# Filler products in the planned gaps of TensorE, a substitution by rows, and held low parts, in a delta-rule attention with two mixture layers

## The chip, the cores and the metric

The kernel runs on one core of one Trainium2 chip. The core has TensorE (PE in the profile, its weight loads PEld), VectorE (DVE), ScalarE (ACT), GpSimd (POOL) and SyncE (SP), which only issues DMAs. The metric is the device time of one execution in microseconds, as a median of several runs; lower is better.

## The reference

Attention by the delta rule over 768 tokens (4 batches, 8 heads, head size 48), then a two-layer network with a leaky ReLU (384 to 2048 to 384), then eight experts (384 to 1024 to 384) whose outputs are weighted by a gate that is normalised by rows and columns in turn.

```python
for t in range(S):                       # attention, per batch and head
    kt, vt, bt = (k_n[:, :, t], v[:, :, t], beta[:, :, t, None])
    y[:, :, t] = np.einsum('bhd,bhde->bhe', q[:, :, t], state)
    v_old = np.einsum('bhde,bhd->bhe', state, kt)
    state = state + bt[:, :, :, None] * np.einsum('bhd,bhe->bhde', kt, vt - v_old)
...
h = x @ w_in                             # first network
x = np.maximum(0.01 * h, h) @ w_out
...
for e in range(E):                       # experts
    h = np.maximum(x @ w1[e], 0.0)
    out += P[:, e:e + 1] * (h @ w2[e])
```

## The kernel before

**Stages.** The 768 tokens are cut into six steps (t = 0 to 5) of 128. For each step and batch b the attention is done in blocks: `part1(t)` normalises the keys and makes the Gram matrix of the step, masked and scaled by beta (tile a, on VectorE, from PSUM); its high half goes to nh (float16, ScalarE), its low half to nl (GpSimd, `tensor_tensor` subtract), and only then GpSimd writes ones on the diagonal of nh (`affine_select`), so nl must be done before that mask. The diagonal 32 x 32 blocks are copied to a_d. `solve(t)` inverts the diagonal blocks of all batches and heads at once on VectorE: it transposes a_d to ld, and for every j multiplies (tile tm) and subtracts (tile xs); in steps 0 and 1 the blocks are 16 wide, so there are 15 such pairs, later 31. A last transpose brings the result to xt (which lies in tile tm). `part2(t, b)` spreads xt into the blocks of a zeroed float16 tile (`spread`: ScalarE, and in step 0 every second block by a VectorE cast), transposes that to a second tile, so that x holds the inverse and u its transpose, and doubles the blocks level by level (s = 16, 32, 64): a product of nh and x, copies p by ScalarE, a product of p and u, copies back into u and x. Then come the products for w, the outputs y and the state.

`main_a(t)` is the first network for the 512 tokens of a step (four batches of 128): 16 slices, each with 9 products x1h/x1l by w into bank ph, leaky ReLUs gh and leak on ScalarE, their difference gl on VectorE, and 9 products into banks po. In step 0 the first four slices (LEAD) run on two batches before the other two are there. `convert` meanwhile brings the weights of the first network into a rounded form by VectorE, ScalarE and GpSimd (tiles raw, cva, cvs, cvp), one piece per slice.

**The order.** All of that (steps 0 to 4 of `main_a`, all six of the attention) is written into a `Recorder`, which doesn't emit instructions but notes them with a cost each (`cost`, L386 on), and then places them: `rank` and `tails` give priorities, attention is favoured by a lead (`AHEAD`), priorities are shaken by random numbers (`SEED`), `place` walks through the engines' queues and takes the best of `ROUNDS` tries; `emit` writes the instructions in the order of their planned starts, and each engine executes in that order. Banks of PSUM are handed out by the plan too (`takes`). In `cost`, the last value marks operations that the plan keeps apart from GpSimd's on VectorE (`shared`). Two loops of products of the zero-filled tile stir into bank ph (`STIR`: 144 and 20) have the lowest rank and are placed wherever PE would idle early on; the tile is later used for maxima. In step 0 the first four subtractions nl are held behind the end of the first solve (`late`, `solved`).

From the last step of the first network on (L1326 and later) another planner orders the work; the change doesn't touch it.

```python
        two = not psum and (method == "tensor_scalar" or len([v for v in src if v.ids.size > 1]) > 1)
...
        for o in late[0:B]:
            o.deps.add(solved[0])
            o.held.add(solved[0])
```

Of the kernel before, what the change touches and what calls it, by code (L numbers as in the profile page):

```python
# [12 lines left out]
F16 = mybir.dt.float16  # L13
# [3 lines left out]
ALU = mybir.AluOpType  # L17
# [3 lines left out]
B, H, S, D = 4, 8, 768, 48  # L21
# [25 lines left out]
SMALL = (0, 1)  # L47

STIR = (145, 20)
AHEAD, EARLY = 60.0, 60.0  # L50
ROUNDS, SEED = 10, 4
NEAR = 0.02
SLACK = 4.0
PAD = 0.07
VTOP = 32.0
# [238 lines left out]
class Recorder:  # L294
# [62 lines left out]
    def cost(eng, method, out, reads, kw):  # L357
# [34 lines left out]
            lat = 0.11 + 0.00073 * n  # L392
        else:
            lat = 0.145 + 0.00104 * m
        two = not psum and (method == "tensor_scalar" or len([v for v in src if v.ids.size > 1]) > 1)
        return lat - 0.08, lat, two

    def rank(self):
# [146 lines left out]
            o.rank = best[1][o]  # L545
        return self.place()

    def emit(self, ordered, hold):
        for o in self.order():
            for fn, args, kw in o.calls:  # L550
                args = [x.real() if isinstance(x, View) else x for x in args]
                o.last = fn(*args, **{k: x.real() if isinstance(x, View) else x for k, x in kw.items()})  # L552
                ordered(o.last)
                for x in o.held:
                    hold(o.last, x.last)
# [3 lines left out]
def delta_moe_kernel(ctx: ExitStack, tc: tile.TileContext, k_l, v_l, q_l, beta_l, wa_in, wg, wc, out):  # L559
# [4 lines left out]
    rec = Recorder()  # L564
# [99 lines left out]
    def spread(t, blk, out, src):  # L664
        if t == 0 and blk % 2:
            dve.tensor_copy(out=out, in_=src)
        else:
            act.activation(out=out, in_=src, func=ACTF.Copy)
# [102 lines left out]
            yield  # L771

    xt_of = {}
    marks, solved = [], []

    def solve(t):
        size = 16 if t in SMALL else 32
# [2 lines left out]
        def blocks(x):  # L780
            return x[:, 0:nd * size * 33].rearrange("p (d r) -> p d r", d=nd)[:, :, 0:size * 32].rearrange(
                "p d (c i) -> p d c i", c=size)[:, :, :, 0:size]
# [3 lines left out]
        xs = a1_p.tile([128, 1056], F32, tag="xs", name="xs")  # L786
        pool.memset(xs, 0.0)
        pool.memset(xs[:, 0:1024:33], 1.0)
        ldb, xsb = blocks(ld).rearrange("p d i c -> p d c i"), blocks(xs)
        yield  # L790
        for j in range(size - 1):
            m = size - 1 - j
            tm = a1_p.tile([128, 1024], F32, tag="tm", name="tm")
            tv = tm[:, 0:nd * (j + 1) * m].rearrange("p (d c i) -> p d c i", d=nd, c=j + 1)
            xv = xsb[:, :, 0:j + 1, j + 1:]
            dve.tensor_tensor(out=tv, in0=ldb[:, :, j:j + 1, j + 1:].to_broadcast([128, nd, j + 1, m]),
                              in1=xsb[:, :, 0:j + 1, j:j + 1].to_broadcast([128, nd, j + 1, m]), op=ALU.mult)
            dve.tensor_tensor(out=xv, in0=xv, in1=tv, op=ALU.subtract)
            if j % 2 == 1:
                yield  # L800
# [5 lines left out]
    def part2(t, b):  # L806
# [15 lines left out]
        xt = xt_of[t]  # L822
        u = at_p.tile([128, H, C], F16, tag="u", name="u")
        x = at_p.tile([128, H, C], F16, tag="x", name="x")
        o = pool.memset(x, 0.0)
        if t == 0 and b < 2:
            behind(o)
        for blk in range(4):
            o = 32 * blk
            spread(t, blk, x[o:o + 32, :, o:o + 32], xt[o:o + 32, :, b * H:(b + 1) * H].rearrange("p j h -> p h j"))  # L830
        dve.transpose(out=u.rearrange("p a b -> p (a b)"), in_=x.rearrange("p a b -> p (a b)"))
        yield
        for s in (16, 32, 64) if t in SMALL else (32, 64):
            pt = p1[b % 2]
# [268 lines left out]
    if True:  # L1103
# [27 lines left out]
        dve.tensor_tensor(out=wg_r[:, :, E:2 * E], in0=wg_f[:, :, 0:E], in1=fr(wg_r[:, :, 0:E]), op=ALU.subtract)  # L1131
        run(solve(0))
        run(part1(1))
        for o in late[0:B]:
            o.deps.add(solved[0])
            o.held.add(solved[0])
        attention(0, 0)
        attention(0, 1)
        ps = phs.tile([128, TB], F32, tag="ph")
        for i in range(2):  # L1140
            for _ in range(STIR[i] // 2):
# [49 lines left out]
            tc.add_manual_dep(ins.ins, before.ins.name, mybir.DependencyInfo(  # L1191
                mybir.DependencyClass.Sync, mybir.DependencyReason.DATA), reason="kept behind")

        rec.emit(ordered, hold)
        pe, act, dve, pool, sp = engines
        ident, ones, wmax, xmax, cmax, wg_f, wg_r, wa, x2_dram = fixed
        x1h, x1l = x1r
# [219 lines left out]
        for c in range(KD):  # L1417
            tag, k = "leak", c % 2

            def emit(c=c, k=k):  # L1420
                o[c] = g_p.slots["leak"][k]
                return [ordered(act.activation(out=o[c], in_=po[c], func=ACTF.Copy))]
# [397 lines left out]
```

## Time and profile before

| | |
|---|---|
| median of 3 runs | 2220.17 us (2218.66 to 2225.01) |
| the profiled execution, time | 2224.42 us |
| its span, first to last instruction | 2222.7 us |
| PE busy | 2108.3 us (95%), 16963 products |
| VectorE busy | 1697.5 us (76%) |
| ScalarE busy | 1399.2 us (63%) |
| GpSimd busy | 607.0 us (27%) |
[...]

The page cuts the span into 40 slices of 55.6 us. PE's busy tenths are 6688 in the first four, 9 or so in the others; the clock's tenths are 8568 in the first four, then 8, 8, and 9 (90% or more) to the end. [...]

### The profile page before, as it was taken

Reading aid. Unit: us, or ns where it says so; the run is one execution under the profiler, and the core shown is the slowest. Engines: PE = TensorE matmul, PEld = TensorE weight load, DVE = VectorE, ACT = ScalarE, POOL = GpSimd, SP = SyncE. Lnnn points to the kernel's source line nnn. Section 1 sums busy time; section 2 is a strip of 40 time slices with the busy share of each in tenths; the row PEclk is TensorE's granted clock in tenths of the full one; section 3 lists DMA queues with packets and bytes.
Section 4 is the critical chain, followed back from the end, with each engine's and each line's share of the span. In section 5 each row is a group of like instructions: output and inputs, shape, how many; then the busy total and the mean of one; then the engine's idle time right before and its main releaser. Section 6 shows DMA issues by size and latency. Waiting matters only on the chain.

```text
span 2222.7 us, 42895 instructions
## 1 busy us (share of the span) xinstructions
PE 2108.3 (95%) x16963; PEld 1585.6 (71%) x16963; DVE 1697.5 (76%) x3313; ACT 1399.2 (63%) x2621; POOL 607.0 (27%) x672
## 2 busy tenths in 40 slices
PE   6688889999999999999999999999999999999999
PEld 4576767787777775767677777777777777777776
DVE  9776687658676467786877877877877878877877
ACT  5868757545656366777666656656656656656554
POOL 3644531103020052345215114214213313312200
PEclk8568889999999999999999999999999999999999
DMA  2456655466655663224333333333333323323321
GB/s 88 141 179 205 220 180 191 167 203 206 200 174 180 220 243 129 108 79 143 114 107 136 115 108 135 115 107 135 115 108 129 121 103 120 123 107 117 112 100 51
DMA packets 123450, 312.85 MB, mean 141 GB/s; under 512 B 14960, under 2 KB 66800, under 8 KB 117104
## 3 DMA queue, kind: packets, MB, share of 16 engines
q1 hardware_dynamic: 121088, 306.18, 40.2%
q10 hardware_dynamic: 2160, 3.93, 0.5%
q8 instruction: 133, 2.18, 0.4%
q14 instruction: 69, 0.57, 0.1%
HBM read 247.84 MB, written 62.13 MB: 139 GB/s over the span
## 4 chain that ended last, share of the span: by engine, by line
PE 75%; DVE 10%; ACT 6%; issue 2%; POOL 2%; DMA 1%; DVEq 0%; ACTq 0%; POOLq 0%; SPq 0%
PE b L1474 25%; PE b L1573 19%; PE ph L1573 10%; PE ph L1474 6%; PE bg L552 5%; PE po L552 4%; PE ph L552 4%; DVE tm L552 2%; DVE xs L552 2%; ACT x L552 2%; DVE gl L552 1%; ACT a_d L552 1%; DVE stir L552 1%; DVE a L552 1%; PE po L1350 1%
## 5 line engine op out<-in xcount | busy, mean ns | idle before, releaser
L1235 POOL TENSOR_TENSOR stg<-stg 128x128 f32<-128x128 f32 (+2 forms) x248 | 166.7, 690 | 805.6 <-ACT stg L1232 801.5
L1474 PEld LDWEIGHTS <-w1h 128*128 128x128 f16 x2112 | 204.8, 98 | 221.0 <-issue 1.7
L1474 PE MATMUL b<-xoh,w1h 128*128 128x512 f16 x864 | 327.5, 379 | 0.0
L1474 PE MATMUL b<-xoh,w1l 128*128 128x512 f16 x864 | 327.5, 379 | 0.0
L1474 PE MATMUL b<-xol,w1h 128*128 128x512 f16 x864 | 327.4, 379 | 0.0
L1238 DVE SCALAR_TENSOR_TENSOR acc<-b,pm,acc 128x192 f32<-128x192 f32 (+1 forms) x357 | 155.6, 449 | 92.4 <-PE b L1573 91.4
L1474 PEld LDWEIGHTS <-w1l 128*128 128x128 f16 x1056 | 103.3, 98 | 124.6
L1232 ACT ACTIVATE b<-b 128x512 f32<-128x512 f32 x144 | 84.2, 584 | 139.3 <-PE b L1474 138.1
L1238 DVE SCALAR_TENSOR_TENSOR acc<-ph,pm,acc 128x192 f32<-128x192 f32 (+1 forms) x231 | 98.1, 433 | 76.9 <-PE ph L1573 76.8
L1232 ACT ACTIVATE c<-b 128x512 f32<-128x512 f32 x192 | 113.8, 593 | 62.7 <-PE b L1474 61.7
L552 PE MATMUL ph<-x1h,w 128*128 128x512 f32 (+1 forms) x504 | 149.6, 412 | 3.1 <-ACT leak L552 2.0
L552 PE MATMUL po<-gh,w 128*128 128x512 f32 (+1 forms) x504 | 141.9, 407 | 10.8 <-ACT gh L552 10.6
L1238 DVE SCALAR_TENSOR_TENSOR c<-c,c 128x512 f32<-128x512 f32 x192 | 135.0, 720 | 6.0 <-ACT c L1232 3.7
L1235 DVE TENSOR_TENSOR c<-c,c 128x512 f32<-128x512 f32 x192 | 136.1, 712 | 2.5
L1238 DVE SCALAR_TENSOR_TENSOR c<-b,v 128x512 f32<-128x512 f32 x144 | 97.6, 689 | 43.7 <-PE b L1474 43.1
L1235 POOL TENSOR_TENSOR w2l<-stg,w2h 128x576 f16<-128x576 f32 (+1 forms) x96 | 108.6, 1151 | 81.4 <-ACT w2h L1232 81.4
L552 PEld LDWEIGHTS po<-gh,w 128*128 128x128 f32 x504 | 92.4, 199 | 28.8 <-ACT gh L552 12.3
L552 DVE TENSOR_TENSOR gl<-leak,gh 128x512 fp32r<-128x512 f32 (+1 forms) x84 | 61.1, 728 | 63.1 <-ACT leak L552 55.1
L552 PEld LDWEIGHTS ph<-x1h,w 128*128 128x128 f32 x504 | 94.5, 202 | 20.5 <-ACT leak L552 2.3
L1235 POOL TENSOR_TENSOR w1l<-stg,w1h 128x384 f16<-128x384 f32 (+1 forms) x64 | 85.9, 1348 | 34.0 <-ACT w1h L1232 34.0
L552 ACT ACTIVATE gh<-ph 128x512 fp32r<-128x512 f32 (+1 forms) x84 | 48.2, 573 | 73.5 <-PE ph L552 71.7
L1232 ACT ACTIVATE b<-ph 128x512 f32<-128x512 f32 x144 | 84.2, 585 | 6.6 <-PE ph L1474 2.5
(511 smaller groups left out, 6670.2 us busy)
## 6 DMA issues: line engine op xcount, KB each, us to landing
w<-wa_scratch SPq DMA_DIRECT2D x100, 768.0 KB, 4.8
acc_scratch<-acc SPq DMA_DIRECT2D x84, 384.0 KB, 2.6
acc<-acc_scratch SPq DMA_DIRECT2D x84, 384.0 KB, 3.5
stg<-wc SPq DMA_DIRECT2D x64, 384.0 KB, 8.7
xoh<-xo_scratch SPq DMA_DIRECT2D x21, 1152.0 KB, 5.1
xol<-xo_scratch SPq DMA_DIRECT2D x21, 1152.0 KB, 8.4
raw<-wa SPq DMA_DIRECT2D x48, 256.0 KB, 2.9
wa_scratch<-cvp SPq DMA_DIRECT2D x48, 256.0 KB, 3.4
```

Source lines behind the costliest of these rows:

```text
L552: o.last = fn(*args, **{k: x.real() if isinstance(x, View) else x for k, x in kw.items()})
L1232: return vec("ACT", n, lambda e: e.activation(out=out, in_=src, func=func, scale=scale), reads, writes, **kw)
L1235: return vec(eng, n, lambda e: e.tensor_tensor(out=out, in0=a, in1=b, op=fn), reads, writes, **kw)
L1238: return vec("DVE", n, lambda e: e.scalar_tensor_tensor(out=out, in0=a, scalar=scalar, in1=b, op0=f0, op1=f1), reads, writes, **kw)
L1350: ordered(pe.matmul(out=po[c], lhsT=self.w[wi][:, DM + c * 128:DM + (c + 1) * 128], rhs=getattr(self, n), start=i == 0 and m == 0, stop=i ...
L1474: ordered(pe.matmul(out=banks[b], lhsT=w[:, a], rhs=x[:, c].rearrange("p s k -> p (s k)"), start=start, stop=i == 2 and (a, c) == terms[-1 ...
L1573: ordered(pe.matmul(out=banks[b][:, 0:HD], lhsT=xx[:, o:o + 128], rhs=wt[:, t], start=first and k == 0 and j == 0, stop=k == NK - 1 and j ...
```

## The change

Five things are changed.

1. *Fillers.* `emit` watches PE's planned gaps. Where a gap is longer than 0.5 us and the next group of products begins a bank, it queues int(0.8 x gap / 0.107) products ahead of that group. They multiply the bits of the identity matrix, read as float16, 128 x 128 by 256 columns, and write the first half of the bank that is about to be begun; the group then overwrites it.
2. *Substitution by rows.* `solve` no longer works down the columns of the blocks but along their rows; the result is the transpose of what it was. `part2` therefore spreads it into u and transposes u to x.
3. *Held low parts.* The four nl of step 0 wait for the transpose of the second batch (`turned[1]`), not for the end of the solve.
4. *A cost rule.* Casts on VectorE (`tensor_copy`) that don't read PSUM are now planned apart from GpSimd's work.
5. *Numbers.* `AHEAD` 60 to 50, `SEED` 4 to 7.

```diff
-AHEAD, EARLY = 60.0, 60.0
-ROUNDS, SEED = 10, 4
+AHEAD, EARLY = 50.0, 60.0
+ROUNDS, SEED = 10, 7
+FILL = 0.5
...
-        two = not psum and (method == "tensor_scalar" or len([v for v in src if v.ids.size > 1]) > 1)
+        two = not psum and (method in ("tensor_scalar", "tensor_copy") or len([v for v in src if v.ids.size > 1]) > 1)
...
-    def emit(self, ordered, hold):
+    def emit(self, ordered, hold, filler):
+        free = 0.0
         for o in self.order():
+            if o.eng == "PE":
+                gap, free = o.start - free, o.start + o.slot
+                if gap > FILL and o.takes and o.rank >= 0:
+                    bank = View(o.takes[0], np.arange(512)).real()
+                    for _ in range(int(0.8 * gap / 0.107)):
+                        ordered(filler(bank[:, 0:256]))
...
-        ldb, xsb = blocks(ld).rearrange("p d i c -> p d c i"), blocks(xs)
+        ldb, xsb = blocks(ld), blocks(xs)
...
-            tv = tm[:, 0:nd * (j + 1) * m].rearrange("p (d c i) -> p d c i", d=nd, c=j + 1)
-            xv = xsb[:, :, 0:j + 1, j + 1:]
-            dve.tensor_tensor(out=tv, in0=ldb[:, :, j:j + 1, j + 1:].to_broadcast([128, nd, j + 1, m]),
-                              in1=xsb[:, :, 0:j + 1, j:j + 1].to_broadcast([128, nd, j + 1, m]), op=ALU.mult)
+            tv = tm[:, 0:nd * (j + 1) * m].rearrange("p (d i c) -> p d i c", d=nd, i=m)
+            xv = xsb[:, :, j + 1:, 0:j + 1]
+            dve.tensor_tensor(out=tv, in0=ldb[:, :, j + 1:, j:j + 1].to_broadcast([128, nd, m, j + 1]),
+                              in1=xsb[:, :, j:j + 1, 0:j + 1].to_broadcast([128, nd, m, j + 1]), op=ALU.mult)
...
-        o = pool.memset(x, 0.0)
+        o = pool.memset(u, 0.0)
...
-            spread(t, blk, x[o:o + 32, :, o:o + 32], xt[o:o + 32, :, b * H:(b + 1) * H].rearrange("p j h -> p h j"))
-        dve.transpose(out=u.rearrange("p a b -> p (a b)"), in_=x.rearrange("p a b -> p (a b)"))
+            spread(t, blk, u[o:o + 32, :, o:o + 32], xt[o:o + 32, :, b * H:(b + 1) * H].rearrange("p j h -> p h j"))
+        turned.append(dve.transpose(out=x.rearrange("p a b -> p (a b)"), in_=u.rearrange("p a b -> p (a b)")))
...
-        for o in late[0:B]:
-            o.deps.add(solved[0])
-            o.held.add(solved[0])
         attention(0, 0)
         attention(0, 1)
+        for o in late[0:B]:
+            o.deps.add(turned[1])
+            o.held.add(turned[1])
...
+        still = fixed[0].bitcast(F16)
+
+        def filler(out):
+            return engines[0].matmul(out=out, lhsT=still[:, 0:128], rhs=still, start=True, stop=True)
```

There are 256 fillers in 27 groups of 4 to 27. Nineteen groups (199 products) stand ahead of the work of step 1's first two batches for the outputs, five (36) in what follows up to the end of step 1's attention, three (21) behind that.

What stands in a row on VectorE behind the first solve, before (tile tm holds the solved blocks; the number after u and x tells the two batches apart: 156 and 158 are batch 0, 157 and 159 batch 1):

```order
L552 STREAM_TRANSPOSE tm_153<-xs_152 128x1024
L552 CAST x_158<-tm_153 32x8x32 x2
L552 CAST x_159<-tm_153 32x8x32 x2
L552 STREAM_TRANSPOSE u_157<-x_159 128x1024
L552 SCALAR_TENSOR_TENSOR a_1_148<-bg_96,beta,upper 128x128
```

and with the change:

```order
L560 STREAM_TRANSPOSE tm_153<-xs_152 128x1024
L560 CAST u_157<-tm_153 32x8x32 x2
L560 CAST u_156<-tm_153 32x8x32 x2
L560 STREAM_TRANSPOSE x_159<-u_157 128x1024
L560 STREAM_TRANSPOSE x_158<-u_156 128x1024
L560 TENSOR_SCALAR cvs_177<-cva_136 128x256
L560 SCALAR_TENSOR_TENSOR a_0_147<-po_98,beta,upper 128x128
```

Batch 1 is spread first and both transposes stand together, ahead of the Gram rows of step 1.

What stands in a row on GpSimd from the masks of step 0 on, before (nl and nh 102 are batch 0, 106 batch 1, 110 and 114 batches 2 and 3):

```order
L552 AFFINE_SELECT mt_155<-mt_155 128x4x128
L552 TENSOR_TENSOR nl_0_107<-a_1_148,nh_0_106 128x1024
L552 TENSOR_TENSOR nl_0_115<-uc_150,nh_0_114 128x1024
L552 TENSOR_TENSOR nl_0_103<-a_0_147,nh_0_102 128x1024
L552 AFFINE_SELECT nh_0_102<-nh_0_102 128x1024
L552 TENSOR_TENSOR cva_136<-cva_136,cvs_177 128x256
```

and with the change:

```order
L560 AFFINE_SELECT mt_155<-mt_155 128x4x128 x2
L560 MEMSET xs_152 128x1056
L560 MEMSET xs_152 128x32
L560 TENSOR_TENSOR nl_0_103<-a_0_147,nh_0_102 128x1024
L560 TENSOR_TENSOR nl_0_107<-a_1_148,nh_0_106 128x1024
L560 TENSOR_TENSOR cva_136<-cva_136,cvs_177 128x256
L560 AFFINE_SELECT nh_0_106<-nh_0_106 128x1024
```

Two subtractions instead of three stand ahead of the first mask, and they now wait for batch 1's transpose.

What stands in a row on ScalarE behind the spreading of the first solve, before (p are the copies of the first level):

```order
L552 ACTIVATE cvs_178<-raw_176 128x256
L552 ACTIVATE a_d_135<-a_1_148 32x32x8 x2
L552 ACTIVATE nh_0_122<-a_1_148 128x1024
L552 ACTIVATE a_d_135<-a_1_148 32x32x8
L552 ACTIVATE cva_136<-cva_136 128x256
L552 ACTIVATE a_d_135<-a_1_148 32x32x8
L552 ACTIVATE p_0_0_132<-bg_94 32x8x16
```

and with the change:

```order
L560 ACTIVATE a_d_135<-a_0_147 32x32x8
L560 ACTIVATE cva_136<-cva_136 128x256
L560 ACTIVATE cvp_179<-cva_136 128x256
L560 ACTIVATE a_d_135<-a_0_147 32x32x8
L560 ACTIVATE a_d_135<-a_1_148 32x32x8
L560 ACTIVATE nh_0_122<-a_1_148 128x1024
L560 ACTIVATE cvp_180<-cva_136 128x256
L560 ACTIVATE p_1_0_133<-po_97 32x8x16
```

The first copy p now stands behind work on both Gram groups a_0 and a_1 of step 1, not behind one.

## Rows read from the trace of the kernel before

**Rows 1.** PE by stretch: us, length, busy (instructions), granted clock, DMA share, GB/s.

```profile
0.00:60.00 60.00, 36.84 (x299) 0.86 0.28 90
60.00:76.00 16.00, 10.39 (x108) 0.79 0.41 130
76.00:120.00 44.00, 32.34 (x314) 0.51 0.44 142
120.00:136.00 16.00, 14.09 (x175) 0.93 0.64 205
136.00:152.00 16.00, 15.97 (x70) 0.50 0.45 157
152.00:200.00 48.00, 33.66 (x309) 0.82 0.68 216
200.00:330.00 130.00, 112.63 (x810) 0.88 0.59 195
330.00:765.00 435.00, 409.75 (x3265) 0.98 0.58 193
```

**Rows 2.** PE's waits from 60 to 200 us, then from 330: total, times, longest.

```profile
PE po L552 <- ACT p L552: 7.5, 2, 7.1
PE po L552 <- ACT gh L552: 6.0, 3, 4.7
...
PE bg L552 <- ACT x L552: 5.3, 5, 2.4
```

**Rows 3.** VectorE's timeline, 18 to 53 us: start, duration, operation, [idle before it].

```profile
18.80 0.60 DVE L552 CAST a_d<-uc 32x256 f16<-32x256 f32 x1
...
41.72 1.25 DVE L552 STREAM_TRANSPOSE tm<-xs 128x1024 f32<-128x1024 f32 x1
43.07 7.96 DVE L552 CAST x<-tm 32x256 f16<-32x256 f32 x4
51.13 1.25 DVE L552 STREAM_TRANSPOSE u<-x 128x1024 f16<-128x1024 f16 x1
```

**Rows 4.** GpSimd's timeline, 43 to 51 us, first subtraction and mask.

```profile
43.05 2.12 POOL L552 TENSOR_TENSOR nl<-a,nh 128x1024 f16<-128x1024 f32 x1 [11.67 <-DVE tm L552]
...
49.68 1.11 POOL L552 TENSOR_SCALAR_AFFINE_SELECT nh<-nh 128x1024 f16<-128x1024 f16 x1
```

**Rows 5.** ScalarE's timeline, 54 to 59 us.

```profile
54.51 1.28 ACT L552 ACTIVATE a_d<-a 32x256 f16<-32x256 f32 x2 [5.83 <-DVE a L552]
...
58.64 0.27 ACT L552 ACTIVATE p<-bg 32x128 f16<-32x128 f32 x1
```

**Rows 6.** PE's timeline, 36 to 66 us.

```profile
36.33 3.01 PE L552 MATMUL ph<-stir 128*128 128x256 f16 x26
...
50.85 0.61 PE L552 MATMUL bg<-x,nh 128*128 128x64 f16 x8 [6.27 <-POOL nh L552]
...
60.70 0.61 PE L552 MATMUL po<-u,p 128*128 128x64 f16 x8 [7.11 <-ACT p L552]
61.13 4.88 PE L552 MATMUL ph<-stir 128*128 128x256 f16 x22
```

**Rows 7.** PE's timeline, 94 to 163 us.

```profile
94.75 0.58 PE L552 MATMUL bg<-u,p 128*128 128x64 f16 x8 [1.87 <-DVE u L552]
...
136.58 3.49 PE L552 MATMUL bg<-uc,mt 128*128 128x48 f32 x16
...
161.64 1.65 PE L552 MATMUL po<-gh,w 128*128 128x512 f32 x3 [4.72 <-ACT gh L552]
```

**Rows 8.** Tile tm, 28 to 43 us: count, ns min/median/max, first and last start.

```profile
L552 DVE TENSOR_TENSOR tm<-ld,xs x15: 191/332/480, 28.1 to 41.2; 128x30 f32<-128x30 f16 x2, 128x56 f32<-128x56 f16 x2, 128x78 f32<-128x78 f16 x2, 128x96 f32<-128x96 f16 x2
L552 DVE TENSOR_TENSOR xs<-xs,tm x15: 152/258/293, 28.7 to 41.5; 128x30 f32<-128x30 f32 x2, 128x56 f32<-128x56 f32 x2, 128x78 f32<-128x78 f32 x2, 128x96 f32<-128x96 f32 x2
```

**Rows 9.** Timelines of GpSimd and VectorE, 68 to 72 us.

```profile
68.77 2.14 POOL L552 TENSOR_TENSOR nl<-a,nh 128x1024 f16<-128x1024 f32 x1
...
69.26 2.40 DVE L552 TENSOR_SCALAR cva<-cva 128x256 f32<-128x256 f32 x4 [3.28 <-ACT cva L552]
```

More of the change, by code (lines that the diff above doesn't have):

```diff
@@ L773, in delta_moe_kernel @@
     xt_of = {}
-    marks, solved = [], []
+    marks, solved, turned = [], [], []
     def solve(t):
@@ L1192, in hold @@
                 mybir.DependencyClass.Sync, mybir.DependencyReason.DATA), reason="kept behind")
-        rec.emit(ordered, hold)
+        still = fixed[0].bitcast(F16)
+        def filler(out):
+            return engines[0].matmul(out=out, lhsT=still[:, 0:128], rhs=still, start=True, stop=True)
+        rec.emit(ordered, hold, filler)
         pe, act, dve, pool, sp = engines
```

## The prediction

> **What bounds the kernel now.** I first read TensorE by stretch [rows 1]. In the first 765 us, the only part that the change rearranges, PE is busy for 665.7 us. Two losses stand beside that. Idle time is 765 - 665.7 = 99.3 us: 23.2 us before 60 us, 33.5 between 60 and 200, 17.4 between 200 and 330, 25.3 in the remaining 435. The second loss is the clock: busy time at a granted clock of 0.5 does half the work, so busy time multiplied by (1 - clock) is what a full clock would have saved. That is 5.2 us before 60, then 2.2 + 15.8 + 1.0 + 8.0 + 6.1 = 33.1 us between 60 and 200, 13.5 between 200 and 330, and 8.2 after. From 330 us on PE is busy for 94% of the time at 0.98. So what can be won lies before 330 us, most of it between 60 and 200.
>
> The waits come next [rows 2]: between 60 and 200 us PE waits longest for ScalarE's copies p (7.5 us in two waits) and gh (6.0 in three), links of the serial chain of step 0. After 330 us no single wait is above 2.4 us. The timelines show where that chain is held. At 43 us VectorE begins four casts that spread the solved blocks, and they take 7.96 us, 1.99 each, while a like cast at 18.80 us took 0.60 beside POOL's fills [rows 3]. At 43.05 POOL begins three low-part subtractions, which end as its mask starts at 49.68 [rows 4]. The casts are slow exactly beside them. VectorE reaches the next Gram rows only after the casts, ScalarE sits idle for 5.83 us for these and copies p, queued behind them, at 58.64 [rows 5]; PE idles 6.27 and then 7.11 us [rows 6].
>
> The clock follows the kind of work. It is 0.5 from 76 to 120 and from 136 to 152 us [rows 1], although PE is nearly always busy in the second: with, among others, 48-column float32 products, 3.5 us for 16 [rows 7]. Between 60 and 76 us it is 0.79 on average, and there 22 products of the zero-filled tile "stir" ran without a break from 61.13 [rows 1, 6]. A stir product takes 3.01/26 = 0.116 us on a full clock and 4.88/22 = 0.222 on a half one [rows 6].
>
> **The change part by part.** The sum is made against the profiled execution (span 2222.7, time 2224.42) and carried over to the median of the runs, 2220.17.
>
> *Substitution by rows.* Same number of instructions and elements; the multiplication no longer reads column j with a stride. In the first solve a multiplication has a median of 332 ns and a subtraction of the same size 258 [rows 8]. If the stride is the whole difference, 15 x 74 ns = 1.1 us goes, on a chain on which VectorE never pauses; if not, nothing. I take **-1** (0 to -1.1). Later solves get shorter too, but PE is fed by the main products there: 0.
>
> *Casts freed, low parts held.* The casts fall to at most 4 x 0.60 = 2.4 us, 5.6 less on VectorE. This isn't 5.6 us for PE. The two subtractions that stand ahead of the first mask now begin after the transpose: 42.0 (41.72 + 1.25 - 1) + 2.4 + 1.25 = 45.6, then two subtractions of about 2.2 (a third of 43.05 to 49.68), one product of the conversion of the weights (0.7 estimated, a third of a subtraction) and the mask of 1.1 (49.68 to the 50.85 of the product behind it): 51.8, so the first level's product is 1 us later than 50.85 [rows 3, 4, 6]. What comes earlier is the next Gram rows (most of the 5.6 us) and the copies p; but the new order on ScalarE puts p behind both Gram groups instead of one, which gives back about half. I expect the next level's product 1 to 2 us before 60.70, and the second batch, whose mask no longer waits for a late POOL, some 3 to 4 earlier. I take **-2** (-6, all that the casts lose, to +3.6, below).
>
> *The transpose now stands ahead of the first product.* For the last two batches of step 0 it adds 1.25 us [rows 3] to each chain, yet before, the second product waited for that same transpose (1.87 us at 94.75 [rows 7]). Cost 0 to 2.5, I take **+1**. In later steps main products cover it; without that cover it would be 20 x 1.25 us, which the 94% after 330 us speaks against.
>
> *Fillers.* 256 products of 256 columns in 27 places; 199 of them stand at places that the trace of before has between 60 and 200 us, 36 between 200 and 330, 21 later. They are 256 x 0.116 = 30 us of PE at full clock, 57 at half. Between 60 and 200 it is 23 to 44 us, against 33.5 us of idle there. Idle time hides them as long as each gap is as long in truth as in the plan (at least 0.134 us per product, from the code's 0.8 and 0.107). [...] I take **+2** for the gaps that turn out short (0 to +17.5, below).
>
> *What the fillers give back.* Full clock in more of the stretch. Of the 33.1 us I take half as regained, as the groups (4 to 27 products) are shorter than the run of 22 that raised the clock at half rate, but many stand close together; of that two thirds shorten the time, since behind PE other waits come up (at 161.64 PE waits 4.72 us for gh [rows 7], a ScalarE queue that a faster PE doesn't shorten). That is 33.1 x 0.5 x 0.67 = **-11**, bounds 0 and -33. Between 200 and 330 us, 36 fillers: 13.5 us lost, a tenth of it, **-1.5**.
>
> *New seed, lead of 50.* The order of steps 0 to 4 is dealt anew, with the same work. Only 5 fillers stand in the last 435 us, so the plan sees PE as full there; the trace has 25.3 us of small waits, the longest 2.4 [rows 1, 2]. Two or three of these more or fewer: **0**, within 6 either way. From 765 us on the code is unchanged.
>
> Sum: -1 - 2 + 1 + 2 - 11 - 1.5 = -12.5; 2220.2 - 12.5 = **2208 us** (own range 2199 to 2213).
>
> [...]
>
> **The rivals.**
> [...] The four held subtractions meet VectorE's weight conversion instead. Beside such a subtraction four scalings took 2.40 us from 69.26 [rows 9]; at the 0.25 us of an undisturbed short one (bounded by the 0.258 of rows 8) they are 1.0: 1.4 lost each, 4 x 1.4 = 5.6 us. For it: the conversion's instructions stand right behind the transposes in the new order. Against: ScalarE's queue may be the later one anyway. The term becomes -2 + 5.6 = +3.6, the time 2214.
>
> *The clock isn't raised.* Groups too short or too far apart: the -12.5 of the two clock terms is gone and 2220 remains. For it: 0.5 all through 76 to 120 us with 73% busy. Against: the zero-filled stirs, the same shape, did raise it.
>
> *Slower: the fillers overrun at half clock.* A filler costs 0.222 us where the plan left 0.134 of gap. If the clock stays at half and real gaps equal planned ones, 199 x (0.222 - 0.134) = 17.5 us; if all 33.5 us of idle could be used, 44.2 - 33.5 = 10.7. With the other terms (-1 - 2 + 1) and no clock gain: +9 to +15.5, 2229 to 2236, middle 2232. It decides from the point where real gaps are under 1.66 times the planned ones while the clock is low. For it: the stirs from 61.13 still took 0.222 us, just where the first groups now stand. Against: the waits of 6 and 7 us there, and that fillers themselves are the work that raised the clock.
>
> *More.* Full clock in the whole stretch and nothing behind it: up to -25, 2187 to 2199.
>
> **How the numbers follow.** A difference under 0.3%, 6.7 us, can't be told from no change: faster is below 2213.5, slower above 2226.8. Chances: forecast 0.52 (0.48 faster, 0.04 same by the reshuffle), more 0.08, lock moved 0.10 (0.04 faster, 0.06 same), clock not raised 0.17 (0.14 same, 0.03 slower), overrun 0.13 (slower). Faster 0.60, same 0.24, slower 0.16. The range 2195 to 2227 leaves out the overrun and most of "more", 0.19.
>
> **What would show it.** Right: casts of 0.4 to 0.6 us behind the first solve; a multiplication as long as a subtraction; a first-level product near 52 us; a mean granted clock above 0.85 between 76 and 160 us with PE idle under 15 us there; the first main product some 8 us earlier, the switch to the hand-planned last step some 12 earlier, and the same length behind it. Wrong: fillers whose first one waits for a bank's reader, product groups at 0.22 us that end later than the real product's inputs; new waits above 2.5 us behind 330 us; the wait for gh moved to a place where a full clock doesn't help.

## The result, and the profile after

The changed kernel takes 2191.73 us (2189.83 to 2194.31), the kernel before took 2220.66 beside it: a ratio of 0.9868 [0.9848, 0.9887], 29 us less. The direction was forecast, the size wasn't: 12.5 us were expected, and the time lies below the range of 2195 to 2227. One execution of e6_old_hold, at a mean granted clock of 0.554, took 3561.92 us and is left out of that run's median below.

All but 1 us of it is gained before the switch to the hand-planned part. The tile cmax is reduced once at the end of each of steps 0 to 4; the row of each kernel gives ns min/median/max, then first and last start. Before:

```profile
L552 DVE TENSOR_REDUCE cmax<-xmax x5: 141/145/156, 329.9 to 769.5; 128x1 f32<-128x3 f32 x5
```

After:

```profile
L560 DVE TENSOR_REDUCE cmax<-xmax x5: 136/146/157, 312.3 to 739.5; 128x1 f32<-128x3 f32 x5
```

17.6 us are won by the end of step 0's network, 30.0 by the end of step 4. Behind that both kernels need the same time within 1 us: 2222.7 - 769.5 = 1453.2 and 2191.7 - 739.5 = 1452.2 us.

TensorE by stretch, against [rows 1], with the same columns:

```profile
0.00:60.00 60.00, 40.91 (x327) 0.86 0.30 95
60.00:76.00 16.00, 10.98 (x164) 1.00 0.57 170
76.00:120.00 44.00, 37.66 (x463) 0.88 0.55 174
120.00:136.00 16.00, 14.28 (x145) 1.00 0.75 242
136.00:152.00 16.00, 12.59 (x86) 0.79 0.54 159
152.00:200.00 48.00, 38.75 (x360) 0.93 0.62 202
200.00:330.00 130.00, 111.50 (x821) 0.95 0.61 200
330.00:765.00 435.00, 419.94 (x3358) 0.99 0.60 201
```

The clock did what was hoped for: 0.51 became 0.88 from 76 to 120 us, 0.50 became 0.79 from 136 to 152, and its mean over the whole span rose from 0.965 to 0.986. Busy time multiplied by (1 - clock) falls from 33.1 to 0 + 4.5 + 0 + 2.6 + 2.7 = 9.8 us between 60 and 200. It is tempting to stop here and call the gain the clock's; the first two experiments show that little of it is.

The places that the prediction named, by TensorE's timeline (start, length, operation, [idle before it]), against [rows 6]:

```profile
53.47 0.61 PE L560 MATMUL po<-x,nh 128*128 128x64 f16 x8 [8.60 <-POOL nh L560]
...
59.12 0.41 PE L560 MATMUL bg<-u,p 128*128 128x64 f16 x8 [1.80 <-ACT p L560]
...
59.58 2.24 PE L1205 MATMUL bg<-ident 128*128 128x256 f16 x19
...
109.82 0.60 PE L560 MATMUL ph<-x1h,w 128*128 128x256 f32 x3
```

The first-level product starts at 53.47 (50.85 before), the next level at 59.12 (60.70), the first main product at 109.82 (115.10). The row at 59.58 is a group of 19 fillers: 2.24/19 = 0.118 us each at a granted clock of 1.00, where the stirs at 61.13 of [rows 6] still took 0.222 at 0.50.

VectorE and GpSimd behind the first solve, against [rows 3, 4]:

```profile
42.33 2.21 DVE L560 CAST u<-tm 32x256 f16<-32x256 f32 x4
...
46.86 1.31 DVE L560 TENSOR_SCALAR cvs<-cva 128x256 f16<-128x256 f32 x1
```

```profile
45.90 4.25 POOL L560 TENSOR_TENSOR nl<-a,nh 128x1024 f16<-128x1024 f32 x2 [2.32 <-DVE x L560]
51.59 0.79 POOL L560 TENSOR_TENSOR cva<-cva,cvs 128x256 f32<-128x256 f32 x1 [1.44 <-DVE cva L560]
52.33 1.09 POOL L560 TENSOR_SCALAR_AFFINE_SELECT nh<-nh 128x1024 f16<-128x1024 f16 x1
```

The four casts take 2.21 us, not 7.96. The subtractions begin at 45.90 (45.6 forecast) and take 4.25 (4.4 forecast), but then GpSimd waits 1.44 us for a piece of the weights' conversion on VectorE, so that the mask starts at 52.33 and the product is 1.7 us later than worked out.

The first solve, against [rows 8]:

```profile
L560 DVE TENSOR_TENSOR tm<-ld,xs x15: 191/267/326, 28.8 to 40.5; 128x30 f32<-128x30 f16 x2, 128x56 f32<-128x56 f16 x2, 128x78 f32<-128x78 f16 x2, 128x96 f32<-128x96 f16 x2
L560 DVE TENSOR_TENSOR xs<-xs,tm x15: 153/257/292, 30.2 to 40.8; 128x30 f32<-128x30 f32 x2, 128x56 f32<-128x56 f32 x2, 128x78 f32<-128x78 f32 x2, 128x96 f32<-128x96 f32 x2
```

A multiplication now has a median of 267 ns (332 before), a subtraction 257. That the order in which the same elements are walked makes a difference of this kind is shown by e10 below, which changes nothing else: 389 ns on average became 517.

### The profile page after: what moved, and what is told of

Read it like the earlier page. It is cut to its first block, busy times and chain, and to the rows that moved or that the text cites. A ratio compares the mean times of both kernels' runs of the same rounds, so it can differ in the third digit from the quotient of the medians.

```text
span 2191.7 us, 43420 instructions
## 1 busy us (share of the span) xinstructions
PE 2100.6 (96%) x17219; PEld 1577.7 (72%) x17219; DVE 1674.5 (76%) x3313; ACT 1399.2 (64%) x2621; POOL 605.7 (28%) x672
## 3 DMA queue, kind: packets, MB, share of 16 engines
q8 instruction: 135, 2.21, 0.4%
## 4 chain that ended last, share of the span: by engine, by line
PE 77%; DVE 10%; ACT 7%; issue 3%; POOL 2%; DMA 1%; SPq 0%; DVEq 0%; ACTq 0%; POOLq 0%
PE b L1487 25%; PE b L1586 19%; PE ph L1586 11%; PE ph L1487 6%; PE bg L560 5%; PE po L560 5%; PE ph L560 4%; ACT u L560 2%; DVE tm L560 2%; DVE xs L560 1%; DVE a L560 1%; ACT p L560 1%; ACT cva L560 1%; DVE gl L560 1%; PE ph L1339 1%
## 5 line engine op out<-in xcount | busy, mean ns | idle before, releaser
L560 PE MATMUL ph<-x1h,w 128*128 128x512 f32 (+1 forms) x504 | 143.5, 400 | 5.3 <-ACT leak L560 5.3
L560 PE MATMUL po<-gh,w 128*128 128x512 f32 (+1 forms) x504 | 137.5, 397 | 0.6 <-ACT gh L560 0.6
```

## Experiments

The theory on record was: the gain is the clock's, given back by the fillers. The rivals that came up: the shorter multiplications, the held low parts, the planner's rule, and the order that the lead and the seed happen to deal. Each ratio is to the kernel before on the same chip; a difference "by the ratios" is that of two ratios, times 2220.66 us. "The order is kept" means that apart from the edit every engine issues the same instructions in the same order; any other edit deals the whole order of steps 0 to 4 anew.

### e1_no_fill: the fillers left out, the order kept

```diff
-FILL = 0.5
+FILL = 1e9
```

> The changed kernel with the gap threshold out of reach: no filler, every other instruction in the same order on every engine. Clock theory (the fillers keep TensorE's granted clock up, and that is nearly the whole gain of 29 us): 15 to 25 us slower than the changed kernel, about 2207 to 2217, the granted clock between 60 and 200 us back near 0.7, busy time x (1 - clock) before the last step back to 45 to 60 us from 24. Order theory (the new order, the freed casts and the rows are the gain and the fillers only stand in idle time): 2190 to 2197, clock little changed or its loss without effect on the end.

2194.39 us, 0.988 [0.9857, 0.9903]: the fillers, and the clock that they raise, are together worth 2.7 us, and the intervals overlap. What the fillers cost and what the clock gives back can't be told apart by this run, since both go at once. The clock was indeed lost. TensorE from 60 to 200 us without the fillers (e1), and then with them (the changed kernel):

```profile
60.00:200.00 140.00, 109.66 (x1048) 0.76 0.61 193
```

```profile
60.00:200.00 140.00, 114.25 (x1213) 0.91 0.60 189
```

From 60 to 110 us, ScalarE (columns: us, length, its busy time, PE's clock, DMA share, GB/s), without the fillers (e1):

```profile
60.00:110.00 50.00, 45.36 (x113) 0.64 0.56 172
```

and with them (the changed kernel):

```profile
60.00:110.00 50.00, 45.45 (x113) 0.90 0.56 172
```

ScalarE is busy for 91% of these 50 us and does the same 113 instructions, whether the clock is 0.64 or 0.90. The first main product starts at 109.86 and 109.82. A slow TensorE there spends its own idle time (without the fillers it is busy for 34.48 of these 50 us), and the first main product doesn't wait for it. Behind that the fillers seem to cost something: in the profiled executions step 0's network ends earlier without them, at 309.4 against 312.3 us, and only step 4 ends later, at 742.1 against 739.5. The ends of the steps in e1:

```profile
L560 DVE TENSOR_REDUCE cmax<-xmax x5: 140/146/156, 309.4 to 742.1; 128x1 f32<-128x3 f32 x5
```

### e2_fill_alone: the fillers alone, added to the kernel before (239 of them), the order kept

```diff
-        rec.emit(ordered, hold)
+        rec.emit(ordered, hold, filler)
```

(with `filler` and the loop in `emit` as in the change)

> The kernel before with the fillers alone (239 of them, in its own plan's gaps): old seed, lead 60, substitution by columns, low parts held behind the solve, casts not kept apart. Clock theory: 2195 to 2205, 15 to 25 us below the kernel before. Order theory: 2214 to 2222. Overrun (fillers longer than the real gaps, above all at half clock): above 2222.

2219.02 us, 0.9984 [0.9969, 0.9999]: 3.6 us less by the ratio (2.4 by the medians), hardly clear of noise. The clock from 60 to 200 us rises from 0.70 on average to 0.91, as with the whole change; TensorE in the kernel before, and then in e2:

```profile
60.00:200.00 140.00, 106.46 (x971) 0.70 0.54 175
```

```profile
60.00:200.00 140.00, 110.11 (x1174) 0.91 0.56 178
```

Here a place can be named where the clock counts. From 136 to 152 us TensorE of the kernel before is busy for 15.97 of 16 us at a clock of 0.50 [rows 1], and VectorE waits for it. With the fillers the clock there is 0.89, and the same operation of VectorE starts 3.7 us earlier (0.6 of that stems from before 136 us). VectorE in the kernel before, and then in e2:

```profile
144.63 0.55 DVE L552 TENSOR_TENSOR v<-v,bg 128x384 f32<-128x384 f32 x1 [1.80 <-PE bg L552]
```

```profile
140.89 0.54 DVE L560 TENSOR_TENSOR v<-v,bg 128x384 f32<-128x384 f32 x1
```

Two kernels give about 3 us for the fillers and the clock together, with an uncertainty of about as much. The theory that they are nearly the whole gain (15 to 25 us) falls.

### e4_f32_fill: longer fillers, the order kept

```diff
-        still = fixed[0].bitcast(F16)
+        still = fixed[0]
-            return engines[0].matmul(out=out, lhsT=still[:, 0:128], rhs=still, start=True, stop=True)
+            return engines[0].matmul(out=out[:, 0:64], lhsT=still, rhs=still[:, 0:64], start=True, stop=True)
```

> The changed kernel, same 256 places, but each filler a float32 product of 64 columns of the identity instead of a float16 one of 256 columns: about the same time on TensorE at full clock. [...]

2245.55 us, 1.0117 [1.0091, 1.0142]: 54 us slower than the changed kernel. The fillers into bg in the changed kernel, the same in e4 (where a filler leaves two records, 450 for 225 fillers), and TensorE's stretch in e4:

```profile
L1205 PE MATMUL bg<-ident 128*128 128x256 f16 x225 | 33.4, 302 | 13.3 <-ACT mt L560 4.5 <-ACT u L560 3.4 <-ACT p L560 2.9
```

```profile
L1205 PE MATMUL bg<-ident 128*128 128x64 f32 x450 | 78.6, 351 | 9.7 <-ACT p L560 2.9 <-ACT mt L560 2.7 <-ACT u L560 2.6
```

```profile
76.00:120.00 44.00, 42.15 (x325) 0.60 0.48 147
```

The time lies above both forecasts. The granted clock from 60 to 200 us is 0.74, below 0.8 as the second one had it, but this doesn't decide between them: the estimate that the fillers are about as long on TensorE as the float16 ones didn't hold. 78.6 us stand in gaps in which those took 33.4. Part of that is the low clock, but where the clock is 1.00 a filler still takes 1.55/6 = 0.26 us, against 0.118:

```profile
276.00 1.55 PE L1205 MATMUL bg<-ident 128*128 128x64 f32 x12 [0.23 <-ACT u L560]
```

From 76 to 120 us TensorE is busy for 96% of the time. So the overrun that the prediction feared does happen with longer fillers. With the float16 ones at most a small part of it shows: without them step 0 ends 2.9 us earlier (e1).

### e3_old_deal, e6_old_hold, e7_old_rule: the changed kernel with one more part undone

```diff
-AHEAD, EARLY = 50.0, 60.0
-ROUNDS, SEED = 10, 7
+AHEAD, EARLY = 60.0, 60.0
+ROUNDS, SEED = 10, 4
```

> The changed kernel with the old seed 4 and lead 60, all else as changed (289 fillers in other gaps). If the new deal of the order is worth nothing by itself, as the prediction had it, 2186 to 2198. If the 12 us that were won after the first step's end are the deal's, 2200 to 2206.

2197.40 us, 0.989 [0.9869, 0.9911].

```diff
-            o.deps.add(turned[1])
-            o.held.add(turned[1])
+            o.deps.add(solved[0])
+            o.held.add(solved[0])
```

> The changed kernel with the low parts of step 0 held behind the end of the solve as before (227 fillers). Rows theory: 2191 to 2197. Freed casts theory: the casts beside the subtractions take 1.5 to 2 us each again and 6 to 10 us come back, 2198 to 2204.

2190.82 us, 0.9877 [0.9847, 0.9906].

```diff
-        two = not psum and (method in ("tensor_scalar", "tensor_copy") or len([v for v in src if v.ids.size > 1]) > 1)
+        two = not psum and (method == "tensor_scalar" or len([v for v in src if v.ids.size > 1]) > 1)
```

> The changed kernel with the old cost rule (casts on VectorE not planned apart from GpSimd; 298 fillers). The casts of the first two batches are kept free by the hold, so only those of batches 2 and 3 can meet GpSimd's work: 2190 to 2198 by either theory; above 2200 if the rule is what frees the chain.

2203.64 us, 0.9921 [0.99, 0.9942]. None of these keeps the order, so each difference (5.7, -0.9 and 11.9 us) is the part undone plus another deal. How much a deal can be is measured below, and all three lie within it: they settle nothing on their parts.

### e8_rows_alone, e5_columns: the rows alone, and all but the rows

e8 is the kernel before with the new `solve` and the new roles of x and u, as in the change; its first line and its last:

```diff
-        ldb, xsb = blocks(ld).rearrange("p d i c -> p d c i"), blocks(xs)
+        ldb, xsb = blocks(ld), blocks(xs)
...
-        dve.transpose(out=u.rearrange("p a b -> p (a b)"), in_=x.rearrange("p a b -> p (a b)"))
+        dve.transpose(out=x.rearrange("p a b -> p (a b)"), in_=u.rearrange("p a b -> p (a b)"))
```

> The kernel before with the substitution by rows alone (u spread, x transposed; low parts held behind the solve, old seed, lead and rule, no fillers). Rows theory: 2203 to 2211. Freed casts theory: 2215 to 2223. The transposes that now stand ahead of the first products cost up to 2.5 us in either.

2207.62 us, 0.9943 [0.9924, 0.9961].

e5 is the changed kernel with the old `solve` and the old roles, the same lines the other way round:

```diff
-        ldb, xsb = blocks(ld), blocks(xs)
+        ldb, xsb = blocks(ld).rearrange("p d i c -> p d c i"), blocks(xs)
...
```

> The changed kernel with the substitution by columns again (and x spread, u transposed, the low parts held behind u's transpose of batch 1); fillers, cost rule, seed and lead as changed; the plan is dealt anew with it. The runs so far leave about 22 us to the rows, the held parts, the rule and the deal. If the rows carry them (the multiplications of the solves up to 28% shorter, which lets gl of the main products come earlier), 10 to 18 us slower than the changed kernel, 2202 to 2210. If the casts freed by holding and by the rule carry them, 2190 to 2197.

2223.84 us, 1.0009 [0.9995, 1.0023], above both of its ranges. In this order nothing is left without the rows. But VectorE's multiplications add up to 70.8 us in e5 (below) and 59.9 in the changed kernel; 11 us less can't give 32 by themselves.

```profile
L560 DVE TENSOR_TENSOR tm<-ld,xs 128x31 f32<-128x31 f16 (+20 forms) x154 | 70.8, 460 | 4.0 <-ACT x L560 1.8
```

Either the exchange of u and x counts, or the order that each is dealt.

### e9_rows_old_roles, e10_slow_rows: multiplications faster or slower, the order kept

e9 is e5_columns with the multiplications by rows; the solved blocks are turned back by a strided read of the transpose:

```diff
-        solved.append(dve.transpose(out=xt.rearrange("p a b -> p (a b)"), in_=xs[:, 0:1024]))
+        solved.append(dve.transpose(out=xt, in_=xs[:, 0:1024].rearrange("p (i c) -> p c i", i=32)))
```

> As e5_columns with the multiplications of the substitution by rows, but the solved blocks turned back by a strided read of the transpose, so that x and u keep the roles of before. PE, ScalarE, GpSimd and SyncE issue the same rows in the same order as in e5_columns (2223.8 us), and VectorE's order is the same too; only the shapes of the multiplications differ. Theory 'short multiplications' (the time is lost in VectorE's queue, by about 11 us of multiplication time in steps 0 to 4 and what waits behind it): tm falls from 70.8 us to about 60 in all, the end of step 4 comes 11 to 30 us earlier than the 770.3 of e5_columns, the time is 2194 to 2213. Rival 'roles and deal' (the gain of the changed kernel comes from u being spread and x transposed, or from the order that these roles are dealt): within 6 us of 2223.8, and step 4 ends within 6 us of 770.

e10 is the changed kernel with the same multiplications, their elements walked in another order:

```diff
-            dve.tensor_tensor(out=tv, in0=ldb[:, :, j + 1:, j:j + 1].to_broadcast([128, nd, m, j + 1]),
-                              in1=xsb[:, :, j:j + 1, 0:j + 1].to_broadcast([128, nd, m, j + 1]), op=ALU.mult)
+            lv, yv, w = ldb[:, :, j + 1:, j:j + 1], xsb[:, :, j:j + 1, 0:j + 1], "p d i c -> p d c i"
+            dve.tensor_tensor(out=tv.rearrange(w), in0=lv.rearrange(w).to_broadcast([128, nd, j + 1, m]), in1=yv.rearrange(w).to_broadcast([128, nd, j + 1, m]), op=ALU.mult)
```

> The changed kernel with one thing undone: the multiplication walks its elements with the row index innermost, so that it reads and writes with a stride again; same results in the same places, new roles of x and u. All five engines issue the rows of the changed kernel in its order; only the shapes of the multiplications differ. Theory 'short multiplications': tm rises from 59.9 us to 70 or more, the end of step 4 moves from 739.5 to 750 to 770, the time is 2202 to 2224. Rival 'roles and deal': within 6 us of 2191.7.

e9: 2215.84 us, 0.9972 [0.996, 0.9983], 8 us under e5. e10: 2209.74 us, 0.994 [0.9925, 0.9955], 18 us over the changed kernel (16 by the ratios). The multiplications in all (busy us, mean ns) of the kernel before:

```profile
L552 DVE TENSOR_TENSOR tm<-ld,xs 128x31 f32<-128x31 f16 (+20 forms) x154 | 72.5, 471 | 2.3 <-ACT x L552 0.3
```

of the changed kernel:

```profile
L560 DVE TENSOR_TENSOR tm<-ld,xs 128x31 f32<-128x31 f16 (+20 forms) x154 | 59.9, 389 | 2.3
```

of e10:

```profile
L560 DVE TENSOR_TENSOR tm<-ld,xs 128x31 f32<-128x31 f16 (+20 forms) x154 | 79.5, 517 | 2.3
```

and of e9, with its strided transposes (ns min/median/max) below, and those of e5 below that:

```profile
L560 DVE TENSOR_TENSOR tm<-ld,xs 128x31 f32<-128x31 f16 (+20 forms) x154 | 55.3, 359 | 4.0 <-ACT x L560 1.8
```

```profile
L560 DVE STREAM_TRANSPOSE tm<-xs x6: 1861/2004/2062, 40.6 to 681.1; 128x1024 f32<-128x1024 f32 x6
```

```profile
L560 DVE STREAM_TRANSPOSE tm<-xs x6: 1201/1245/1246, 41.2 to 688.7; 128x1024 f32<-128x1024 f32 x6
```

e10 has 19.6 us more on VectorE and takes 16 to 18 us more. e9 has 70.8 - 55.3 = 15.5 us less in multiplications and 6 x (2.00 - 1.24) = 4.6 more in transposes, 10.9 less, and takes 8.2 less. So a microsecond of the solves costs about 0.8 at the end, in both directions (8.2/10.9 and 16/19.6). It comes up step by step: in the profiled executions e10 ends step 0 only 2.8 us after the changed kernel (315.1 against 312.3) but step 4 15.0 after it (754.5 against 739.5), as its theory had it. e9 ends step 4 7.8 us before e5 (762.5 against 770.3), between its theory and the rival, and its time lies in neither range. The ends of the steps in e10:

```profile
L560 DVE TENSOR_REDUCE cmax<-xmax x5: 141/150/155, 315.1 to 754.5; 128x1 f32<-128x3 f32 x5
```

It is TensorE's small waits that grow: from 330 to 735 us PE is busy for 392.74 of 405 us in the changed kernel and for 381.62 in e10, and from 330 to 740 its longest sum of waits, for gl, goes from 3.8 us in 3 to 6.1 in 5 (TensorE from 330 to 735 us, the changed kernel and then e10):

```profile
330.00:735.00 405.00, 392.74 (x3244) 1.00 0.60 199
```

```profile
330.00:735.00 405.00, 381.62 (x3168) 1.00 0.57 189
```

Shown with that is the price of 0.8 in two orders. If it holds for the change too, some 10 of its 12.6 us of shorter multiplications (72.5 to 59.9) come through; this is an estimate. Still open after it: e9 and the changed kernel need VectorE equally long for multiplications and these transposes (55.3 + 6 x 2.00 and 59.9 + 6 x 1.24 us, 67.3 each) and lie 24 us apart.

### e11_deal_alone, e12, e13, e14, e15: other orders of the same work

```diff
-ROUNDS, SEED = 10, 7
+ROUNDS, SEED = 10, 3
```

(and 4, 9, 29; the kernel before with the lead of 50 and seeds 7 and 4)

> The kernel before with the new lead and seed only (50 and 7). Theory 'a deal is worth what it happens to be worth': anywhere within 8 us of 2220.7, and not the 5.7 us that the same two numbers are worth in the changed kernel. Rival 'the lead is worth it': 2215, 5 to 6 us faster, as between e3_old_deal (2197.4) and the changed kernel (2191.7).

> The changed kernel dealt with seed 3 in place of 7; nothing else differs. Theory 'deal' (24 us between the changed kernel and e9_rows_old_roles are mostly the order that was dealt): seeds scatter by 10 us or more, so 2190 to 2212 here. Rival 'roles' (u spread, x transposed, is what gains): 2188 to 2200, within 8 us of 2191.7, as e3_old_deal with 2197.4.

> The changed kernel dealt with seed 4 in place of 7, at the lead of 50. Theory 'deal': 2190 to 2212. Rival 'roles': 2188 to 2200.

> e9_rows_old_roles (substitution by rows, old roles of x and u, at most 4.6 us of longer transposes) dealt with seed 3. Theory 'deal': one of the two seeds falls below 2205 and the gap to the changed kernel with the same seed is under 10 us. Rival 'roles': 2208 to 2224, 12 us or more above the changed kernel with the same seed.

> e9_rows_old_roles dealt with seed 4. Theory 'deal': one of the two seeds falls below 2205 and the gap to the changed kernel with the same seed is under 10 us. Rival 'roles': 2208 to 2224, 12 us or more above the changed kernel with the same seed.

> The changed kernel dealt with seed 9. Theory 'deal': the changed kernel's orders lie at 2198 with a scatter of some 7 either way, so 2188 to 2206 here, and no better than 2191.7 with more than an even chance. Rival 'seed 7 is the typical order and 3 an outlier': 2189 to 2195.

> The changed kernel dealt with seed 29. Theory 'deal': 2188 to 2206. Rival: 2189 to 2195.

> The kernel before with the lead of 50 and its own seed 4. Theory 'rows and rest are worth about 20 us in any deal, the deal adds the rest': 2212 to 2226, above every order of the changed kernel. Rival 'the 29 us are nearly all deal': below 2206.

| kernel | lead/seed | us | ratio to before |
|---|---|---|---|
| changed | 50/7 | 2191.73 | 0.9868 [0.9848, 0.9887] |
| changed (e14) | 50/9 | 2192.31 | 0.9866 [0.9847, 0.9884] |
| changed (e12) | 50/4 | 2198.41 | 0.9889 [0.9868, 0.991] |
| changed (e3) | 60/4 | 2197.40 | 0.989 [0.9869, 0.9911] |
| changed (e14) | 50/29 | 2197.93 | 0.9896 [0.9873, 0.9919] |
| changed (e12) | 50/3 | 2205.74 | 0.9925 [0.9906, 0.9944] |
| old roles (e13) | 50/4 | 2194.36 | 0.9876 [0.9857, 0.9896] |
| old roles (e13) | 50/3 | 2212.18 | 0.995 [0.9931, 0.9968] |
| old roles (e9) | 50/7 | 2215.84 | 0.9972 [0.996, 0.9983] |
| before | 60/4 | 2220.66 | 1 |
| before (e11) | 50/7 | 2217.67 | 0.9972 [0.9961, 0.9983] |
| before (e15) | 50/4 | 2211.42 | 0.9948 [0.9932, 0.9965] |

By the ratios the deal is worth 13 us among six orders of the changed kernel, 21 among three of its old-role twin, 12 among three of the kernel before (e15 lies just under the 2212 that was its lowest forecast). With seed 4 the twin is as fast as the changed kernel, so the exchange of u and x isn't what makes the 24 us. Over the three seeds the twin is on average 8.6 us slower, part of it by its longer transposes; a few us for the exchange can't be excluded. And e5's 2223.8 is mostly its order: the twin has that same order, and is the slowest of its three. Seeds 9 and 29 were picked because the planner itself ends early with them, so the six aren't a blind draw. None is measurably faster than the changed kernel.

Worked out from the table: the mean ratio is 0.9889 for the changed kernel and 0.9973 for the kernel before, 0.0084 or 18.7 us apart. The changed kernel's own order is 0.0021 (4.7 us) better than its mean, and the order of before 0.0027 (5.9 us) worse than its mean. That makes 29.3 us. So some 19 us belong to the edits, with a standard error of about 4 us (an estimate from the scatter of so few orders), and some 11 to the two deals. Of the 19, about 10 are the multiplications and about 3 the fillers, at prices measured with the order kept. The remaining 6 or so may be the hold, the rule, the exchange of u and x or the scatter; they stay open.

## Why the prediction was wrong in size

**Fillers and clock, +2 - 11 - 1.5.** This step failed, and with it the reason given for the forecast. What the fillers do to the clock was right: 0.88 between 76 and 120 us, the first group at full clock. So was, roughly, the half of 33.1 us that the term took as regained: by busy time x (1 - clock) from 60 to 200 us, the fillers regain 22 us in the old order (106.46 x 0.30 against 110.11 x 0.09 in e2) and 16 in the new one (109.66 x 0.24 in e1 against 114.25 x 0.09). What failed is the step from there to the time, that two thirds of it shorten the path: the sum of -10.5 for fillers and clock measured about -3. One view that would have said so is the other engine in the same stretch. The prediction saw a ScalarE queue behind TensorE at 161.64 us, but nowhere read ScalarE's busy share from 60 to 110 us, which is 89% in the kernel before:

```profile
60.00:110.00 50.00, 44.43 (x109) 0.60 0.44 140
```

In that stretch the lower clock cost idle time that was there anyway (e1). From 136 to 152 us, at 0.50, it did not (e2), but in the new order TensorE is no longer busy throughout there (12.59 of 16 us). The +2 for gaps that turn out short is shown by no run by itself; e1 and e2 show the fillers' cost and the clock's gain only together, as some 3 us less.

**Later solves, 0.** This failed too, by some 9 us (the 10 estimated above, less the 1 forecast for the first solve). "PE is fed by the main products there" rested on PE's 94% [rows 1]. Its 25 us of small waits were seen, and set aside because no one of them was long [rows 2]. The view that speaks is the chain of waits by stretch. From 110 to 765 us, shares by engine and line. The kernel before:

```profile
by line: PE bg L552 17.1%; PE ph L552 13.9%; PE po L552 13.0%; DVE tm L552 8.0%; DVE xs L552 5.6%; ACT x L552 5.2%; issue 4.5%; DVE gl L552 3.4%; ACT a_d L552 2.6%; DVE stir L552 2.5%; DVE a L552 2.4%; DVE cva L552 1.9%; ACT p L552 1.8%; AC
```

The changed kernel:

```profile
by line: PE bg L560 16.0%; PE po L560 15.5%; PE ph L560 14.3%; DVE tm L560 5.1%; ACT u L560 4.9%; issue 4.9%; DVE xs L560 4.5%; DVE a L560 2.5%; DVE gl L560 2.4%; ACT p L560 2.2%; DVE stir L560 2.2%; DVE cva L560 1.9%; ACT cva L560 1.8%; PE
```

In the kernel before, 8.0% of these 655 us, 52 us, are operations of the solves that write tm and that the end waits for: multiplications and last transposes, which take 72.5 + 6 x 1.24 = 79.9 us in all. TensorE works beside them; that its small waits are where the chain comes back is a likely reading, but not shown. The share of their time that lies on the chain, 52/79.9 = 0.7, was at hand before, and it says that the term isn't 0. It is no exact price: in the changed kernel the share is 33/67.3 = 0.5, and yet e10 loses 0.8 us there for each microsecond added. Much was left beside a PE that is busy for 94% of 435 us [rows 1]: from the end of step 0's network to that of step 4 the kernel before takes 769.5 - 329.9 = 439.6 us, the changed kernel 739.5 - 312.3 = 427.2. At the price that e9 and e10 give, a part of these 12.4 us is VectorE's multiplications, by estimate.

**New deal, 0 within 6.** The bound failed. It took the reshuffle as two or three small waits more or fewer; the orders of each kernel above scatter by 12 to 21 us, and two of them, the old one below its kernel's average and the new one above, add 11.

So of 29 us the fillers and the clock make about 3 (10.5 in the sum), the multiplications about 10 (1 in the sum), the deals about 11 (0 in the sum), and some 6 stay open. That the time fell, as forecast, is owed mostly to terms that the sum had near 0; in that the right direction was luck.

**What held.** The multiplication as long as a subtraction in the first solve (-1). The casts at 2.21 us ("at most 2.4") and the next level 1.6 us earlier (1 to 2 forecast). The second batch's first level came at 64.17 against 69.30 before, 5.1 us earlier, more than the 3 to 4 forecast; but the first-level product came 1.7 us later than worked out, for a wait on VectorE's conversion that the sum hadn't, and the first main product 5.3 us earlier, not 8. The same length behind the switch.

The price of the transpose ahead of the first product, +1, wasn't measured by itself; from 60 to 200 us PE waits 3.3 us in three for x. PE's longest wait there is one of a filler for its bank, 3.4 us, which the prediction had among its signs of being wrong:

```profile
PE bg L1205 <- ACT mt L560: 3.4, 1, 3.4
PE bg L560 <- DVE x L560: 3.3, 3, 1.5
```

In the changed kernel these fillers begin at 144.19, and the group behind them starts at 146.49:

```profile
144.19 2.51 PE L1205 MATMUL bg<-ident 128*128 128x256 f16 x11 [3.37 <-ACT mt L560]
146.49 1.06 PE L560 MATMUL bg<-ident,y 128*128 128x128 f32 x4
```

In e1, without them, the bank comes free later, but the group starts at 146.03, half a microsecond earlier:

```profile
146.03 1.18 PE L560 MATMUL bg<-ident,y 128*128 128x128 f32 x4 [1.17 <-ACT mt L560]
```

**The rivals.** "The clock isn't raised" was wrong in its mechanism and nearly right in its price: the clock was raised, and fillers and clock together are worth about 3 us. That the held subtractions meet VectorE's conversion (0.10 among the chances) shows in VectorE's time: beside the one that GpSimd begins at 45.90 a scaling takes 1.31 us (at 46.86, above), beside the one at 64.34 another takes 1.65, where others take 0.28 or 0.29.

```profile
64.97 1.65 DVE L560 TENSOR_SCALAR cva<-cva 128x256 f32<-128x256 f32 x1 [1.74 <-ACT cva L560]
```

That is 2.4 us of the 5.6 that the rival named; what it cost at the end isn't shown. "Overrun" needs the longer fillers of e4. "More" named a range that holds the measured time, for a reason that didn't hold; its "up to -25" doesn't fit its own 2187, which is 33 us below 2220.

## What to carry to other kernels

Cost a clock, or any saving on one engine, by the stretch in which it falls: if another engine is busy for nine tenths there, as here from 60 to 110 us, the saving may buy only idle time. Read the chain of waits by stretch for every operation that a change shortens, even beside an engine that is 94% busy; its share on the chain tells whether the term may be put at 0, and gives a first estimate of the part that comes through (0.7 here, with 0.8 measured in other orders, but 0.5 in the changed kernel). And where a planner deals the order anew at each edit, deal both kernels several times before a difference of ten microseconds is put down to an edit, or make the edit with the order kept.

## What the hardware showed unexpectedly

In these runs the order in which VectorE walks the same elements sets its price: the same 154 multiplications take 389 ns on average in the changed kernel, walked along the row, and 517 in e10, where both the float16 operand and the output are walked with a stride; the 128x1024 float32 transpose takes 2.00 us in place of 1.24 with a strided read (e9, e5). At a granted clock of 1.00 a float32 filler of 64 columns took 0.26 us in e4, a float16 one of 256 columns 0.118 in the changed kernel. And from 76 to 120 us TensorE was granted 0.60 in e4, busy for 42.15 of the 44 us, and 0.88 in the changed kernel, busy for 37.66.
